# Fused attention and two expert stages: second products at four places of a unit, copies out of PSUM first in a step, the queries' split two steps sooner

## The chip, the cores and the metric

One core of one Trainium2 chip runs the whole program. The metric is device microseconds of one execution. The kernel before took 1058.69 us, the median of 3 runs (1058.37 to 1059.4).

## The reference

Attention over 4 batches, 8 heads, 576 positions and a head size of 64, with a bias that a small two-layer network makes of the relative position; then a dense layer with a rational activation, and a routed layer of 8 experts with one expert per token. Everything is fp32. Only attention bears on the change:

```
scores = q @ k.T / sqrt(64) + bias        # 576 x 576 for each batch and head
attn   = exp(scores - rowmax) / rowsum
out    = attn @ v                         # 576 x 64
h = out @ w_in ; g = rational(h) ; x = g @ w_out          # later stages, not touched
out[token] = gate * relu(x @ w1[e]) @ w2[e]
```

## The kernel before, in words

Attention handles two heads of one batch at a time. Such a pair is called a unit: 16 units, numbered u. A unit has nine steps, numbered j = 0 to 8: eight tiles of 128 queries, taken alternately from the two heads (`ORD`), and a ninth that holds the 64 remaining queries of both heads. The loop at L524 runs over all steps, `g = 9 * u + j`, and each turn issues work for several tiles at once, so that a tile passes through the engines over some turns. The order is written out by hand: nothing reorders it. Each engine takes its own instructions in that order, and waits at the head of its queue until what the instruction needs is there. TensorE is PE in the profile, VectorE is DVE, ScalarE is ACT, GpSimd is POOL, and SyncE (SP) issues the loads and stores.

In a turn the code issues, from the top:

- loads by SP: q and k of unit u + 2 at steps 0 to 5 (`load_unit`, L527), v at step 1 (`load_v`);
- `recip` of tile g - 3: on DVE an add and a reciprocal (L363, L364), on POOL a spread to 64 columns (`rb`, L366);
- `expo` of tile g - 2 on ACT (L351);
- `pend`: what the turn before has left to be copied out of PSUM. That is `stack_evac` (L297), `rest_evac` (L420) and `av_evac` (L440);
- `trans_pe` of tile g - 4 on PE (L393: the weights `e`, transposed; L396 and L397: a remainder and the reciprocals) and its copy out of PSUM by ACT (`trans_evac`, L370);
- `scores` of tile g on PE (L330);
- `stack_pe` on PE (L289, L291, L293, L294): q and k of the next unit are transposed, in five pieces that `STACK` assigns to steps 0, 1, 2, 3 and 7; their copies follow in the next turn: piece 4 by DVE (L302, L303), POOL (L304) and ACT (L305), pieces 0 and 2 by ACT (L307), pieces 1 and 3 by DVE (L310, L311);
- the second products, attention times v (`av_pe`, L436), for the unit before. Five chunks c of keys, for two ranges of queries: n = 0 (256 columns, steps in `AV0`) and n = 1 (320 columns, steps in `AV1`). They take 64 columns of the array for each head, and every product is two passes. After the last chunk DVE scales the result out of PSUM (`av_evac`, L445);
- `rowmax` of tile g - 1 on DVE (L346), which also frees the PSUM tile of the scores;
- `split_q` for unit u + 2 on POOL (L263, L265, L268): q is cut into a high and a low part, in four instructions;
- one part of the conversion of weights for a later stage (`CONV`, `conv`): on DVE L61, L62, L67, L70, L76, on ACT L65, on POOL L78 and L80 after L76, on SP loads and stores.

PSUM has two tiles of each kind. The transposes of `trans_pe` and `stack_pe` share the kind "tr": a unit asks for 14 of them in turn, so each needs the copy of the one before the last. In the order of a unit: T5 (the transposes of tile 5, issued in step 0), S4 (piece 4), T6, S0, T7, S1, T8, S2, T0, T1, T2, T3, S3, T4. T7 so needs T6's copy, and T5 needs S3's. Scores have the kind "sc" (a tile's scores need the `rowmax` of the tile two before), and the second products, the remainders and the reciprocals the kind "av".

Of the kernel before, what the change touches and what calls it, by code (L numbers as in the profile page):

```python
# [88 lines left out]
def attention(ctx, tc, k, ins):  # L89
# [121 lines left out]
    def load_bias(p, j):  # L211
        bt = ap.tile([P, S], F32, name="bias_s", bufs=11)
        t = ORD[j]
        for hd in (t // 4,) if t < 8 else range(2):

            n, lanes = (P, bt) if t < 8 else (S - 4 * P, bt[64 * hd:64 * hd + 64])
            r = t % 4 * P if t < 8 else 4 * P
            d = bias_d[r // P][0:n, 2 * p + hd, S - r:2 * S - r]
            for lo, hi, to in ((512, S, 0), (0, 512, 64)) if 4 <= t < 8 else ((0, S, 0),):
                nc.sync.dma_start(lanes[:, to:to + hi - lo], bass.AP(d.tensor, d.offset + lo, [[2 * H * S - 1, n], [1, hi - lo]]))  # L220
        bias_s[p, t] = bt

    def load(dst, src, hd, rem, near):

        if rem:
            nc.sync.dma_start(dst[64 * hd:64 * hd + 64, 8], src[512:576])
        else:
            load_chunks(dst[:, 4 * hd:4 * hd + 4], src[0:512], near)
# [8 lines left out]
    def load_unit(u, i):  # L237
        p, b = divmod(u, B)
        if i == 0:
            r = units[u] = K()  # L240
            r.u, r.p, r.b = u, p, b
            r.qn = xq.tile([P, 9, D], F32, name="qn")
            r.kn = xq.tile([P, 9, 2, D], F32, name="kn")
        r = units[u]
        hd, i = divmod(i, 3)
        dst, src = ((r.qn, ins["q"]), (r.kn[:, :, 0], ins["k"]), (r.kn[:, :, 1], ins["k"]))[i]
        for rem in range(2):
            load(dst, src[b, 2 * p + hd], hd, rem, i == 0)

    def load_v(u):  # L250
        r = units[u]
        r.vn = ap.tile([P, 8, D], F32, name="vn")
        for hd in range(2):
            h = 2 * r.p + hd
            load_chunks(r.vn[:, 4 * hd:4 * hd + 4], ins["v"][r.b, h, 0:512], True)
            nc.sync.dma_start(vrem[u % 2][64 * hd:64 * hd + 64, hd], ins["v"][r.b, h, 512:576])
# [92 lines left out]
    def expo(g):  # L349
        e, st = tiles[g][0:2]  # L350
        nc.scalar.activation(e, e, AF.Exp, bias=st[:, 0:1], scale=-1.0, accum_out=st[:, 1:2])  # L351
        if g % 9 == 8:
            both = tiles[g][3]
            nc.gpsimd.tensor_scalar(both[:, S:S + 64], e[:, 512:576], 1.0, 1.0, ALU.mult, ALU.mult)
# [3 lines left out]
    def recip(g):  # L358

        n = 1 if g % 9 == 8 else 2  # L360
        if g % 9 % 2 or n == 1:
            st = tiles[g][4]
            nc.vector.tensor_scalar(st[:, 2, 0:n], st[:, 1, 0:n], 1e-9, None, ALU.add)  # L363
            nc.vector.reciprocal(st[:, 3, 0:n], st[:, 2, 0:n])  # L364
            rb = recips[g] = ap.tile([P, 2, D], F32, name="rb")
            nc.gpsimd.tensor_scalar(rb, st[:, 3, 0:n].unsqueeze(2).to_broadcast([P, 2, D]), 1.0, 1.0, ALU.mult, ALU.mult)  # L366
# [8 lines left out]
    def trans_pe(g):  # L375
        u, j = divmod(g, 9)
        t = ORD[j]
        r = units[u]
        both = tiles[g][3]
        if j == 0:  # L380
            r.aT = [None, None]
            r.aR = [None, None]
            r.rem = [None, None]
        if j in (0, 4):
            w = Q1 if j == 0 else S - Q1
            n = j // 4
            r.aT[n] = ap.tile([P, 2, 4, w], F32, name=f"aT{n}", bufs=1)
            r.aR[n] = ap.tile([P, 2, w], F32, name=f"aR{n}", bufs=1)
            r.rem[n] = pst.tile([P, 512], F32, name="av")
        ps = r.tps = pst.tile([P, 512], F32, name="tr")  # L390
        for c in range(4):
            e0 = c // 2 * 2 * P + (640 if 4 <= t < 8 else 0)
            nc.tensor.transpose(ps[:, c * P:(c + 1) * P], both[:, e0 + c % 2:e0 + 2 * P:2], k.idf)  # L393
        if j % 2:
            n, q0 = t % 4 // 2, t % 2 * P
            nc.tensor.transpose(r.rem[n][:, Q1 + q0:Q1 + q0 + P], both[:, 512:640], k.idf)  # L396
            nc.tensor.transpose(r.rem[n][:, q0:q0 + P], recips.pop(g).rearrange("p a n -> p (a n)"), k.idf)  # L397
# [16 lines left out]
    def rest_pe(g):  # L414
        both = tiles.pop(g)[3]
        av0, rb = units[g // 9].av0, recips.pop(g)
        nc.tensor.transpose(av0[:, 384:512], both[:, 512:640], k.idf)
        nc.tensor.transpose(av0[:, 256:384], rb.rearrange("p a n -> p (a n)"), k.idf)
# [49 lines left out]
    def first_split(r, p):  # L468
        nc.gpsimd.tensor_scalar(r.xh[p], r.x[p], 1.0, 1.0, ALU.mult, ALU.mult)
        nc.vector.tensor_tensor(r.xl[p], r.x[p], r.xh[p].bitcast(F32), ALU.subtract)  # L470
# [45 lines left out]
    CONV = {0: [(6, -1), (8, -1), (1, 0), (2, 0)], 1: [(3, 0), (7, -1), (0, 1)], 2: [(4, 0)], 3: [(5, 0)], 4: [(6, 0)],  # L516
            5: [(1, 1), (8, 0)], 6: [(7, 0), (3, 1), (2, 1), (0, 2)], 7: [(4, 1)], 8: [(5, 1)]}
    STACK = {0: 4, 1: 0, 2: 1, 3: 2, 7: 3}
    SPLIT = {6: (0,), 7: (1,), 8: (2, 3)}
    AV0 = {0: (0, 1), 1: (2,), 2: (3, 4)}  # L520
    AV1 = {4: (0, 1), 6: (2,), 7: (3,), 8: (4,)}
    pend = []
    setup = routing_setup(tc, k, ins)
    for g in range(NG + 6):  # L524
        u, j = divmod(g, 9)
        if u + 2 < NU and j < 6:
            load_unit(u + 2, j)  # L527
        if 2 <= u < NU and j == 1:
            load_v(u)

        if u + 2 < NU and u % B == 2 and j in (3, 7):
            load_bias(u // B + 1, j // 4)
        w, i = divmod(g - 2, 9)
        if g > 2 and w % B == B - 1 and w + 1 < NU and i >= 2:
            load_bias(w // B + 1, i)
        if g == 3:
            load_bias(0, 8)
        if 12 <= g < 21 or g in (28, 30, 32, 34, 36):
            next(setup)
        if g in later:  # L540
            later[g]()
        if 0 <= g - 3 < NG:
            recip(g - 3)
        if 0 <= g - 2 < NG:
            expo(g - 2)
        for f in pend:
            f()
        pend = []
        if 0 <= g - LAG < NG:
            trans_pe(g - LAG)  # L550
            trans_evac(g - LAG)
        if g < NG:
            scores(g)
        if g - LAG >= 0 and (g - LAG) % 9 == 8 and g - LAG < NG:
            rest_pe(g - LAG)
            pend.append(lambda g=g: rest_evac(g - LAG))
        if u + 1 < NU and j in STACK:
            i = STACK[j]
            ps = stack_pe(u + 1, i)
            pend.append(lambda u=u, i=i, ps=ps: stack_evac(u + 1, i, ps))  # L560
        if 0 <= u - 1 < NU - 1 and j in AV1:
            for c in AV1[j]:
                av_pe(u - 1, 1, c)
            if j == 8:
                pend.append(lambda u=u: av_evac(u - 1, 1))
        if 0 <= g - 1 < NG:
            rowmax(g - 1)
        if u + 2 < NU and j in SPLIT:
            for i in SPLIT[j]:
                split_q(u + 2, i)  # L570
        v = u - 1
        if 0 <= v < NU and j in AV0:
            for c in AV0[j]:
                av_pe(v, 0, c)
            if j == 2:
                pend.append(lambda v=v: av_evac(v, 0))
        for part, d in CONV[j]:
            if 0 <= 2 * u + d < 32:
                conv(2 * u + d, part)
        if g == NG - 6:  # L580
            x0 = first_x()
        if NG - 4 <= g < NG:
            first_split(x0, g - (NG - 4))
        if NG <= g < NG + 3:
            first_mm(x0, g - NG)

        n = g - NG
        if n == 2:
            g_of_h = Rational(nc, k)
            for c in range(2):  # L590
                k.st[c].q = g_of_h.open(1, lambda name: ap.tile([P, S], F32, name="bias_s", bufs=11)[:, 0:k.NB].unsqueeze(1))
            q0, q1 = k.st[0].q, k.st[1].q
            g_of_h.first(q0, 0, k.st[0].h)
            g_of_h.den(q0)
            g_of_h.poly(q0, 0, k.st[0].h)
        if n == 3:
            g_of_h.inv(q0)
            g_of_h.first(q1, 0, k.st[1].h)
            g_of_h.den(q1)
            g_of_h.quot(q0)  # L600
        if n == 4:
            for c in range(5):
                av_pe(NU - 1, 1, c)
            av_evac(NU - 1, 1)
            g_of_h.high(q0, x0.g[0].unsqueeze(1))
            g_of_h.inv(q1)
            g_of_h.poly(q1, 0, k.st[1].h)
            g_of_h.low(q0, x0.g[1].unsqueeze(1))
            g_of_h.quot(q1)
            g_of_h.high(q1, x0.g[2].unsqueeze(1))  # L610
            g_of_h.low(q1, x0.g[3].unsqueeze(1))
# [964 lines left out]
```

## Time and profile before

| | |
|---|---|
| median of 3 runs | 1058.69 us |
| profiled execution, its own time | 1060.23 us |
| its span (first to last instruction) | 1058.5 us |
| busy: PE, PEld, DVE, ACT, POOL | 96%, 84%, 71%, 62%, 26% |
| units of attention | about 64 us to 380 us of the span |

Busy PE is not PE at its peak: its matmuls are pipelined and their ends are modelled. The weight loads (PEld) show better when PE was held: each matmul has one ahead of it. A "<-" names what ended the idle time ahead of an instruction; "issue" means nothing that the profile shows. In a timeline a row is the start, the duration and the instruction, with the number of equal ones that are drawn together; the starts of two rows that follow each other closely are the better measure of what an instruction costs its engine, since the durations overlap by up to 0.1 us.

### The profile page before, as it was taken

The page shows a single profiled execution, that of the slowest core. Times are in us where ns is not written, and L with a number is a line of the kernel's source. Part 1 is how long each engine was busy: PE and PEld are TensorE (multiplying, and loading weights), DVE is VectorE, ACT ScalarE, POOL GpSimd, SP SyncE. Part 2 cuts the span into 40 slices and gives each one's busy share as a digit, 9 for nine tenths or more (in the row PEclk, how much of TensorE's full clock was granted, in tenths as well). Part 3 has the DMA queues.
Part 4 walks back from the last instruction along what each step waited for, and adds up shares of the span by engine and source line. Part 5 has one row for each costly group of instructions (what it writes and reads, how often), then busy time and mean ns, then how long its engine had stood idle before and what let it go on. Part 6 is the DMA issues. An engine that isn't in the chain of part 4 may idle for free. (4 is left out here: it accounts for less than half of the span.)

```text
span 1058.5 us, 19117 instructions
## 1 busy us (share of the span) xinstructions
PE 1016.0 (96%) x6804; PEld 886.1 (84%) x6804; DVE 754.0 (71%) x1548; ACT 651.7 (62%) x1283; POOL 276.0 (26%) x445
## 2 busy tenths in 40 slices
PE   6989999999999999999999999999997999999995
PEld 4667777777777779999999999999997889999982
DVE  7988898888888858888888888888886522111210
ACT  6878788887888857676676767766764422222221
POOL 3434343344343210202103012021051443112200
PEclk9999999999999999999999999999998999999998
DMA  6886885774663318005103112042150366311100
GB/s 174 298 264 163 234 251 169 220 218 127 183 193 101 122 47 324 30 1 22 39 1 31 31 19 43 1 23 67 62 100 1 30 167 232 113 42 40 51 31 18
DMA packets 122072, 113.34 MB, mean 107 GB/s; under 512 B 65055, under 2 KB 94495, under 8 KB 121952
## 3 DMA queue, kind: packets, MB, share of 16 engines
q1 hardware_dynamic: 117828, 101.53, 35.8%
q0 software_dynamic: 3728, 10.25, 3.1%
q8 instruction: 61, 1.00, 0.4%
q14 instruction: 59, 0.48, 0.2%
q10 hardware_dynamic: 396, 0.08, 0.0%
HBM read 78.09 MB, written 33.79 MB: 106 GB/s over the span
## 5 line engine op out<-in xcount | busy, mean ns | idle before, releaser
L759 PE MATMUL sc<-gh,w_b 128*128 128x384 f32 x752 | 208.7, 338 | 1.2 <-ACT x L766 1.2
L759 PEld LDWEIGHTS sc<-gh,w_b 128*128 128x128 f32 x752 | 138.6, 189 | 1.8 <-ACT x L766 1.8
L759 PE MATMUL sc<-gl,w_b 128*128 128x384 f32 x376 | 127.1, 338 | 0.0
L393 PEld LDWEIGHTS tr<-idf,e 128*128 128x128 f32 x576 | 81.0, 207 | 49.1 <-issue 24.9
L351 ACT ACTIVATE e<-e,st 128x576 f32<-128x576 f32 x144 | 112.2, 779 | 14.1 <-DVE st L346 12.1
L370 ACT COPY aT<-tr 128x512 f32<-128x512 f32 x144 | 84.4, 586 | 44.5 <-PE tr L393 42.7
L346 DVE CUSTOM_DVE_ANT_0 e<-sc,bias_s 128x576 f32<-128x576 f32 x144 | 107.6, 748 | 5.4 <-PE sc L330 3.8
L1096 DVE SCALAR_TENSOR_TENSOR hl<-tr,hh 128x256 fp32r<-128x256 f32 x56 | 23.8, 425 | 121.5 <-ACT hh L1095 121.5
L671 PE MATMUL tr<-kn,w_a 128*128 128x384 f32 x372 | 107.0, 342 | 0.1
L393 PE MATMUL tr<-idf,e 128*128 128x128 f32 x576 | 105.1, 305 | 1.7 <-DVE kk L311 0.9
L330 PE MATMUL sc<-kk,qS 128*128 128x288 f32 x512 | 99.0, 315 | 0.4 <-DVE st L346 0.4
L660 ACT CAST gh<-t 128x768 fp32r<-128x768 f32 x47 | 39.2, 835 | 92.7 <-DVE t L656 92.7
L436 PE MATMUL av<-aT,vn 128*64 128x320 f32 (+1 forms) x512 | 82.8, 424 | 0.0
L1086 PE MATMUL tr<-kn,w_a 128*128 128x256 f32 x448 | 81.5, 280 | 0.8 <-DVE hl L1096 0.5
L330 PEld LDWEIGHTS sc<-kk,qS 128*128 128x128 f32 x512 | 72.9, 191 | 1.7 <-PE tr L289 0.5
L759 PEld LDWEIGHTS sc<-gl,w_b 128*128 128x128 f32 x376 | 71.1, 189 | 0.0
L1086 PEld LDWEIGHTS tr<-kn,w_a 128*128 128x128 f32 x448 | 69.7, 188 | 1.7 <-ACT w_b L1131 0.7
L1107 PE MATMUL sc<-w_a,hh 128*128 128x512 f32 x224 | 70.9, 393 | 0.0
L671 PEld LDWEIGHTS tr<-kn,w_a 128*128 128x128 f32 x372 | 68.0, 188 | 2.6 <-issue 2.3
L867 POOL DMA_INDIRECT tab<-ids,si x18 | 23.0, 1275 | 180.0 <-DVE cum L863 165.6
L366 POOL TENSOR_SCALAR rb<-st 128x128 f32<-128x128 f32 x80 | 23.9, 299 | 171.4 <-DVE st L364 155.9
L649 ACT ACTIVATE r<-q,one 128x768 f32<-128x768 f32 x47 | 44.1, 939 | 33.8 <-DVE q L645 33.8
(306 smaller groups left out, 2534.1 us busy)
## 6 DMA issues: line engine op xcount, KB each, us to landing
bias_d<-bo SPq DMA_DIRECT2D x36, 295.5 KB, 4.2
kn<-in_k_dram SPq DMA_DIRECT2D x64, 128.0 KB, 3.6
cst<-in_moe_w_out_dram SPq DMA_DIRECT2D x16, 512.0 KB, 3.9
wo_d<-cvw SPq DMA_DIRECT2D x16, 512.0 KB, 2.9
cst<-in_moe_w_in_dram SPq DMA_DIRECT2D x16, 512.0 KB, 4.8
w_b<-wo_d SPq DMA_DIRECT2D x16, 512.0 KB, 8.0
w_b<-in_moe_w_dram SPq DMA_DIRECT2D x16, 512.0 KB, 8.3
x_d<-xr SPq DMA_DIRECT2D x18, 256.5 KB, 11.7
```

The source lines that it names most:

```text
L330: nc.tensor.matmul(ps[:, hf, 0:HF], st, mv[:, hf * HF:(hf + 1) * HF], start=n == 0, stop=n == last)
L346: nc.vector.tensor_tensor_reduce(out=ev, in0=ps[:, :, 0:HF], in1=bv, scale=-1.0, scalar=3.0e38, op0=ALU.add, op1=ALU.min, accum_out=st[:, ...
L351: nc.scalar.activation(e, e, AF.Exp, bias=st[:, 0:1], scale=-1.0, accum_out=st[:, 1:2])
L370: nc.scalar.copy(dst, src)
L393: nc.tensor.transpose(ps[:, c * P:(c + 1) * P], both[:, e0 + c % 2:e0 + 2 * P:2], k.idf)
L436: nc.tensor.matmul(r.av[64 * hd:64 * hd + 64, 0:w], st, mv, start=c == 0, stop=c == 4)
L649: nc.scalar.activation(q.r, q.q, AF.Ln, bias=self.one[:, 0:1], scale=1.0)
L660: self.nc.scalar.copy(gh, q.t)
L671: nc.tensor.matmul(h[:, 0:k.NB], k.wi[f][:, wv, dc * P:(dc + 1) * P], xv[dc], start=n == 0, stop=n == 11)
L759: nc.tensor.matmul(r.acc[dc][:, 0:NB], wo[f][:, wv, ws], gv, start=f == 0 and n == 0, stop=f == NF - 1 and n == 2)
L1086: nc.tensor.matmul(ps[:, 0:n], w[:, wv, cs], xv[dc // 2][:, dc % 2], start=j == 0, stop=j == 11)
L1107: nc.tensor.matmul(r.acc[a], r.h[f][hv][:, cs], wa[8 + f][:, wv], start=f == 0 and n == 0, stop=f == 7 and n == 2)
```

## The change

Four tables and one order change. The second products of a unit are issued at four steps in place of seven: chunk 2 of range 0 goes from step 1 to step 0, and chunks 3 and 4 of range 1 go from steps 7 and 8 to step 6; the scaling of range 1 and the store that follows it come two turns sooner. The queries' split is issued at steps 4, 5, 6 and 7 in place of 6, 7 and 8, and for that the loads of both heads' q come at steps 0 and 1. The copies that the turn before has left (`pend`) stand ahead of `recip` and `expo`.

```
-    SPLIT = {6: (0,), 7: (1,), 8: (2, 3)}
-    AV0 = {0: (0, 1), 1: (2,), 2: (3, 4)}
-    AV1 = {4: (0, 1), 6: (2,), 7: (3,), 8: (4,)}
+    SPLIT = {4: (0,), 5: (1,), 6: (2,), 7: (3,)}
+    LOAD = (0, 3, 1, 2, 4, 5)
+    AV0 = {0: (0, 1, 2), 2: (3, 4)}
+    AV1 = {4: (0, 1), 6: (2, 3, 4)}
...
-            load_unit(u + 2, j)
+            load_unit(u + 2, LOAD[j])
...
             later[g]()
+
+        for f in pend:
+            f()
+        pend = []
         if 0 <= g - 3 < NG:
             recip(g - 3)
         if 0 <= g - 2 < NG:
             expo(g - 2)
-        for f in pend:
-            f()
-        pend = []
...
-            if j == 8:
+            if j == 6:
                 pend.append(lambda u=u: av_evac(u - 1, 1))
```

## Rows read from the trace of the kernel before

**Rows 1.** Windows: stretch, its length, each engine's busy us, PEclk, DMA share, GB/s.
```profile
200.00:300.00 100.00, 99.69 (x731) 76.02 (x729) 85.86 (x234) 80.52 (x182) 40.43 (x76) 1.00 0.65 184
```

**Rows 2.** Timeline of PEld, one unit: start, us, instruction, idle before and releaser.
```profile
301.16 0.56 PEld L393 LDWEIGHTS tr<-idf,e 128*128 128x128 f32 x4 [0.38 <-issue]
...
303.25 0.55 PEld L393 LDWEIGHTS tr<-idf,e 128*128 128x128 f32 x4 [0.39 <-issue]
...
308.17 0.58 PEld L330 LDWEIGHTS sc<-kk,qS 128*128 128x128 f32 x4
...
310.15 0.56 PEld L393 LDWEIGHTS tr<-idf,e 128*128 128x128 f32 x4 [0.49 <-ACT qS L307]
...
310.84 0.56 PEld L330 LDWEIGHTS sc<-kk,qS 128*128 128x128 f32 x4
311.35 0.57 PEld L393 LDWEIGHTS tr<-idf,e 128*128 128x128 f32 x4
311.83 0.58 PEld L330 LDWEIGHTS sc<-kk,qS 128*128 128x128 f32 x4
...
313.26 0.56 PEld L393 LDWEIGHTS tr<-idf,e 128*128 128x128 f32 x4 [0.49 <-ACT aT L370]
...
314.46 0.49 PEld L291 LDWEIGHTS tr<-idf,kn 128*128 128x128 f32 x4
...
318.94 0.56 PEld L330 LDWEIGHTS sc<-kk,qS 128*128 128x128 f32 x4
...
320.84 0.56 PEld L393 LDWEIGHTS tr<-idf,e 128*128 128x128 f32 x4 [0.39 <-issue]
```

**Rows 3.** Timeline of DVE in the same unit.
```profile
312.36 0.69 DVE L67 SCALAR_TENSOR_TENSOR cvt<-cst,cvt 128x512 uint32<-128x512 uint32 x1
...
315.23 0.69 DVE L310 CAST kk<-tr 128x512 fp32r<-128x512 f32 x1 [0.62 <-PE tr L291]
...
318.38 0.49 DVE L445 TENSOR_TENSOR xs<-av,aR 128x320 f32<-128x320 f32 x1 [0.73 <-PE av L436]
...
319.46 0.42 DVE L61 TENSOR_SCALAR cvt<-cst 128x512 uint32<-128x512 uint32 x1
319.92 0.69 DVE L62 SCALAR_TENSOR_TENSOR cvt<-cst,cvt 128x512 uint32<-128x512 uint32 x1
```

**Rows 4.** Timeline of DVE from step 8 of unit 0 to step 1 of unit 1.
```profile
77.76 0.67 DVE L310 CAST kk<-tr 128x512 fp32r<-128x512 f32 x1
...
79.07 0.75 DVE L346 CUSTOM_DVE_ANT_0 e<-sc,bias_s 128x576 f32<-128x576 f32 x1
...
80.79 0.48 DVE L61 TENSOR_SCALAR cvt<-cst 128x512 uint32<-128x512 uint32 x1
81.30 1.11 DVE L62 SCALAR_TENSOR_TENSOR cvt<-cst,cvt 128x512 uint32<-128x512 uint32 x1
82.33 0.15 DVE L363 TENSOR_SCALAR st<-st 128x2 f32<-128x2 f32 x1
...
82.91 0.29 DVE L303 TENSOR_TENSOR kk<-tr,kk 128x128 fp32r<-128x128 f32 x1
```

**Rows 5.** Timeline of POOL in that stretch.
```profile
80.25 0.74 POOL L78 TENSOR_TENSOR cvw<-cvt,cvw 128x256 fp32r<-128x256 f32 x1 [0.42 <-DVE cvw L76]
80.94 0.92 POOL L80 TENSOR_TENSOR cvw<-cvt,cvw 128x256 fp32r<-128x256 f32 x1
```

**Rows 6.** Timeline of ACT in that stretch.
```profile
81.69 0.78 ACT L351 ACTIVATE e<-e,st 128x576 f32<-128x576 f32 x1
...
83.29 0.27 ACT L305 CAST qrem<-tr 128x128 fp32r<-128x128 f32 x1 [0.74 <-DVE kk L303]
83.45 0.59 ACT L370 COPY aT<-tr 128x512 f32<-128x512 f32 x1
```

**Rows 7.** Timeline of PEld in that stretch: piece 0 behind L305.
```profile
83.61 0.40 PEld L289 LDWEIGHTS tr<-idr,qs 128*128 128x128 f32 x4 [0.19 <-ACT qrem L305]
```

**Rows 8.** Source line L305, all 16 units: what ended ACT's idle time before it (us, times).
```profile
  DVE kk L303: 10.0, 16
```

## The prediction

> **What bounds the kernel now.** I read the page first (the table above): PE is busy 96% of the span, and the change touches only attention, so next the windows. In a window of mid-attention [rows 1] PE shows 99.69 of 100 us, but its weight loads only 76.02, DVE 85.86 and ACT 80.52; the granted clock is 1.00. PE's figure hides gaps, so I went to the timeline of the weight loads over one unit [rows 2]. The unit starts with T6's loads at 301.16 and comes round at 320.84: 19.68 us. The idle times in it are only those beside second products, 0.38 or 0.49 ahead of the next transposes, always the same size, whatever the profile names as releaser ("issue", an ACT copy). So these are no waits for another engine: PE runs through its queue at its own pace, and PE bounds the unit. DVE is the next busiest, and waits for PE at two kinds of places [rows 3]: L310 for the transposes of k (0.62), L445 for the second products (0.73). Last I looked at who stands close behind PE: ACT's L305 waits for DVE's L303 in all 16 units [rows 8], and PE's piece S0 waits for L305 in the first of them, starting 0.05 after its end (83.56 to 83.61) [rows 6, 7].
>
> **Part 1, fewer places.** From scores to the next transposes PE takes 0.51 us with no second products between (310.84 to 311.35), 1.43 with one chunk (311.83 to 313.26), 1.98 with two (308.17 to 310.15) [rows 2]. A chunk so costs 0.55 and a place 0.92 - 0.55 = 0.37 beside it. Three places go, and I take the same 0.37 for the one with 256 columns: 1.11 us less in a unit of PE, 18.57, if nothing else holds it. The chunks themselves stay and move: 0.55 each from steps 7 and 8 to step 6, about 0.43 (0.55 x 256 / 320, an estimate) from step 1 to step 0. Their inputs are ready by then, since the last copies into aT and aR come in step 4 at the latest.
>
> What moves with them: L445 now stands at the head of DVE's step 7 and waits for three chunks. T3 would come at 313.26 + 2 x 0.55 = 314.36 on the clock of rows 2, while L67 of step 6 is done at 313.05 [rows 3], so DVE stands idle some 1.3 us. Behind L445 queue the `rowmax` of tile 6 (L346), L70 and L310. Nobody needs these sooner than L310 needs S3: S3 is 1.20 behind T3 [rows 2], L310 0.77 behind S3's start (314.46 to 315.23) [rows 2, 3], together 1.97; the three in front take 0.49 + 0.75 + 0.69 = 1.93 [rows 3, 4] (L70 taken like L67). So this wait costs nothing, but it leaves nothing over. The stores of the result are issued earlier on SP, with no reader inside attention.
>
> **Part 2, what PE runs into.** Steps 7, 8 and 1 lose their second products on PE, and DVE's work there stays. I follow it from S3 (step 7) to the next thing that PE needs from it.
>
> S3's start to L310: 0.77. L310 to the end of L303: in the first unit DVE runs through just this list without a wait (L310, L311, `rowmax` 7, L76, `rowmax` 8, L61, L62, one add and reciprocal, L302, L303), from 77.76 to 82.91 + 0.29 = 83.20: 5.44 us [rows 4]. The new order puts one `recip` in (behind L311) and one out (behind L303), equal ones, so 5.44 stays. L305 starts 0.09 later, the next ACT instruction 0.16 after it [rows 6]. In the new order that one is the exponential of tile 8, 0.78, and only then comes the copy of T6, 0.59 [rows 6]. PE follows 0.05 behind a copy [rows 7]. Sum 0.09 + 0.16 + 0.78 + 0.59 + 0.05 = 1.67. T7 needs T6's copy, as the tr tiles go in turn. From T7 to the next S3 PE's queue takes 314.46 - 303.25 = 11.21 [rows 2], and with two chunks more 12.31. The circle S3, DVE, ACT, T7, S3 is 0.77 + 5.44 + 1.67 + 12.31 = 20.19 us. That is more than PE's 18.57 and 0.51 more than the 19.68 of before.
>
> The same stretch holds PE once more, inside the circle: scores of step 0 need `rowmax` 7, which ends 0.77 + 1.31 (77.76 to 79.07) + 0.3 (add and reciprocal; 82.33 to 82.91, less L302) + 0.75 = 3.13 after S3's start [rows 2 to 4], 3.18 with the 0.05; PE would be there after 318.94 - 314.46 = 4.48 less two places of 0.92, 2.64. This 0.54 adds nothing, since T6 still ends before ACT gets to its copy.
>
> **Part 3, copies first.** Of the 1.67 above, the exponential's 0.78 is new: before, it stood ahead of L305 and filled ACT's wait for L303. On DVE, L302 gains the time of a `recip`, 0.3. In steps 2 and 4 ACT's copies (L307, `rest_evac`) come sooner by one exponential, which nothing waits for now (no PE idle time beyond the fixed ones [rows 2]). Net, 0.5 worse, in the circle.
>
> **Part 4, split and loads.** POOL is busy 40.43 of 100 us [rows 1]. Four instructions move two steps ahead; the transposes that read them come in the next unit. They now stand ahead of L78 and L80 in steps 4 and 5, so L61 and L67 of steps 5 and 6 may find POOL at work; up to some 0.4 each (below), hidden in the 1.3 us at L445. SP issues as many loads as before in other order; q is there three steps ahead of the split, and k of the first head comes a step or two later for use in the next unit. I take 0; without that cover it would be up to 0.8 a unit.
>
> **The term I had to choose.** L61 and L62 in step 0 took 1.62 us in the first unit (80.79 to 82.41) [rows 4], 1.15 in a later one (319.46 to 320.61) [rows 3]. In the first unit L78 and L80 were running beside them, L80 itself 0.92 in place of 0.74 [rows 5]; in the later one L445's wait had let POOL finish. L78 starts behind L76, and in the new order L76, `rowmax` 8 and L61 stand back to back as in the first unit, so I take 1.62. The ends are 1.15 (circle 19.72) and L61 waiting for both POOL instructions: L61 starts 0.54 after L78, the two last 0.69 + 0.74, and L61 ends 0.28 behind (81.27 against 80.99), so 1.89 with L62 (circle 20.46).
>
> The Trainium skill ("SBUF — State Buffer", section "Who interferes with whom") says that VectorE and GpSimd share a pair of SBUF ports as an exclusive lock for a whole instruction, and counts VectorE instructions with two SBUF inputs in. The trace agrees: L62 took 1.11 beside L80 and 0.69 alone. By that rule the circle is 20.19 or 20.46, without it 19.72.
>
> **Sum.** The trace is of an execution of 1060.23 us (span 1058.5), 1.5 above the median; attention's units in it are regular, so the difference is put on the median. Fourteen passages between units 1 and 15 at +0.51: +7.1. The first passage already has the crowded pattern: 0. The last unit has no S3, and keeps the three places' gain: -1.1. Together +6.0: 1064.7 (1066.2 on the profiled execution's own scale).
>
> **Rivals.**
> - *T7 is not held, PE stays the bound (faster).* It decides at one place: whether T6's copy is done when PE has finished S0. For: ACT has 20% idle time [rows 1]. Against: the wait of L305 for L303 in every unit [rows 8], with the exponential behind it. If only the scores' wait of 0.54 stays, the unit is 18.57 + 0.54 = 19.11 and 15 units give 8.6: 1050.1; if nothing stays, 15 x 1.11 = 16.7: 1042. The Trainium skill ("TensorEngine Tiling (Array Packing)", "Key Properties") says that changing the tiling mode drains TensorE. By it each place removed pays whatever the neighbours do, which is the 1042; the fixed 0.37 a place agrees.
> - *POOL is out of the way in step 0 (no change).* Circle 19.72: 14 x 0.04 - 1.1 = -0.5, 1058.2. For: 1.15 is the row of most later units' shape. Against: it came with DVE's wait at L445, which moves to step 7.
> - *POOL goes first with both (slower still).* Circle 20.46: 14 x 0.78 - 1.1 = +9.8, 1068.5.
>
> **Chances.** Forecast 0.54, POOL first 0.12, POOL away 0.17, T7 not held 0.17. Changes under 0.2% (2.1 us) can't be told from none here. Slower 0.65, the first two; same 0.17; faster 0.18. The range reaches from below the case without POOL to above the heavy one and leaves out the faster rival: 1056 to 1070; the likeliest case alone has 1062 to 1068.
>
> **What would show it.** Right: T7's loads (L393 in step 2) with 0.4 to 1 us of idle time and an ACT copy as releaser; scores of step 0 behind L346; L62 of step 0 near 1.1; L445 in step 7 with more than 1 us of wait; a unit near 20.2. Wrong: no idle time ahead of T7 and a unit near 18.6 to 19.1 (parts 2 and 3 fall), or L62 of 0.69 in step 0 with a unit near 19.7 (only the chosen term falls).

## The result, and the profile after

The changed kernel took 1066.05 us (median of 4 runs, 1065.95 to 1067.82) against 1058.53 for the kernel before in the same runs: ratio 1.0069, 95% interval 1.0053 to 1.0084. It is slower by 7.5 us; the forecast was 1064.7. The profiled execution took 1065.97 us, 5.7 above the one of before.

PE is still busy nearly all the time by the page, and spends less on second products, but the window of mid-attention now shows it held: PE 95.47 of 100 us where [rows 1] have 99.69, and DVE 91.11 where they have 85.86.

```profile
200.00:300.00 100.00, 95.47 (x714) 75.24 (x712) 91.11 (x229) 78.29 (x180) 44.17 (x75) 1.00 0.64 181
```

The timeline of the weight loads (start, duration, instruction, idle time before it and releaser), from step 7 of one unit to T7 of the next and on to the next S3, answers to [rows 2]:

```profile
301.39 0.49 PEld L291 LDWEIGHTS tr<-idf,kn 128*128 128x128 f32 x4
...
303.36 0.58 PEld L393 LDWEIGHTS tr<-idf,e 128*128 128x128 f32 x4
303.85 0.15 PEld L396 LDWEIGHTS av<-idf,e 128*128 128x128 f32 x1
304.36 0.14 PEld L397 LDWEIGHTS av<-idf,rb 128*128 128x128 f32 x1 [0.36 <-POOL rb L366]
304.56 0.56 PEld L330 LDWEIGHTS sc<-kk,qS 128*128 128x128 f32 x4
...
306.90 0.56 PEld L393 LDWEIGHTS tr<-idf,e 128*128 128x128 f32 x4 [0.38 <-ACT cvq L65]
...
308.07 0.40 PEld L289 LDWEIGHTS tr<-idr,qs 128*128 128x128 f32 x4
309.31 0.56 PEld L393 LDWEIGHTS tr<-idf,e 128*128 128x128 f32 x4 [0.84 <-ACT aT L370]
...
321.61 0.49 PEld L291 LDWEIGHTS tr<-idf,kn 128*128 128x128 f32 x4
```

T7 (309.31) sat idle 0.84 us behind ACT's copy. In step 0, T5's last part (L397, 304.36) waited 0.36 behind POOL's spread reciprocals. From S3 to S3 it is 321.61 - 301.39 = 20.22 here; the median over units 10 to 14 is in the table of the next section.

The other side of the circle, DVE, then ACT, then POOL in the same stretch; these answer to [rows 4], [rows 6] and [rows 5].

```profile
302.16 0.69 DVE L310 CAST kk<-tr 128x512 fp32r<-128x512 f32 x1
...
303.49 0.16 DVE L363 TENSOR_SCALAR st<-st 128x2 f32<-128x2 f32 x1
...
303.76 0.74 DVE L346 CUSTOM_DVE_ANT_0 e<-sc,bias_s 128x576 f32<-128x576 f32 x1
...
304.43 0.42 DVE L76 CAST w_a<-cvt 128x512 fp32r<-128x512 f32 x1
...
305.44 0.55 DVE L61 TENSOR_SCALAR cvt<-cst 128x512 uint32<-128x512 uint32 x1
306.02 1.12 DVE L62 SCALAR_TENSOR_TENSOR cvt<-cst,cvt 128x512 uint32<-128x512 uint32 x1
...
307.37 0.29 DVE L303 TENSOR_TENSOR kk<-tr,kk 128x128 fp32r<-128x128 f32 x1
```
```profile
307.75 0.27 ACT L305 CAST qrem<-tr 128x128 fp32r<-128x128 f32 x1 [1.28 <-DVE st L363]
307.92 0.78 ACT L351 ACTIVATE e<-e,st 128x576 f32<-128x576 f32 x1
...
308.69 0.57 ACT L370 COPY aT<-tr 128x512 f32<-128x512 f32 x1
```
```profile
304.01 0.30 POOL L366 TENSOR_SCALAR rb<-st 128x128 f32<-128x128 f32 x1 [3.58 <-DVE st L364]
304.93 0.74 POOL L78 TENSOR_TENSOR w_a<-cvt,w_a 128x256 fp32r<-128x256 f32 x1 [0.62 <-DVE w_a L76]
305.63 0.96 POOL L80 TENSOR_TENSOR w_a<-cvt,w_a 128x256 fp32r<-128x256 f32 x1
```

S3 to L310 0.77, L310 to the end of L303 (307.66) 5.50, L305 0.09 later, then 0.17, 0.77, 0.57 and 0.05 to T7: 1.65 for the five. T7 to S3 321.61 - 309.31 = 12.30. The forecast's four terms were 0.77, 5.44, 1.67 and 12.31. The profile names L363 as L305's releaser, where [rows 8] name L303; L305 still starts 0.09 behind L303's end, so I read the same wait, with L363 merely running beside it by then. The scores of step 0 (304.56) start 0.06 behind the end of `rowmax` 7 (L346, 303.76 + 0.74).

### The profile page after: what moved, and what is told of

Same layout as the page of the kernel before. It is cut to its first block, busy times and chain, and to the rows that moved or that the text cites. A ratio compares the mean times of both kernels' runs of the same rounds, so it can differ in the third digit from the quotient of the medians.

```text
span 1064.2 us, 19112 instructions
## 1 busy us (share of the span) xinstructions
PE 1009.7 (95%) x6804; PEld 890.3 (84%) x6804; DVE 775.8 (73%) x1548; ACT 648.2 (61%) x1283; POOL 289.5 (27%) x445
## 5 line engine op out<-in xcount | busy, mean ns | idle before, releaser
L393 PEld LDWEIGHTS tr<-idf,e 128*128 128x128 f32 x576 | 81.2, 206 | 39.3 <-ACT aT L370 19.0
L393 PE MATMUL tr<-idf,e 128*128 128x128 f32 x576 | 101.3, 299 | 10.7 <-ACT aT L370 9.9
L346 DVE CUSTOM_DVE_ANT_0 e<-sc,bias_s 128x576 f32<-128x576 f32 x144 | 107.1, 745 | 2.3 <-PE sc L330 1.4
L370 ACT COPY aT<-tr 128x512 f32<-128x512 f32 x144 | 83.7, 581 | 31.8 <-PE tr L393 30.3
L436 PE MATMUL av<-aT,vn 128*64 128x320 f32 (+1 forms) x512 | 76.0, 418 | 0.0
L656 DVE SCALAR_TENSOR_TENSOR t<-t,coef,r 128x768 f32<-128x768 f32 x47 | 47.6, 1014 | 24.2 <-ACT r L652 24.2
```

Of the source, the lines that this page charges most:

```text
L346: nc.vector.tensor_tensor_reduce(out=ev, in0=ps[:, :, 0:HF], in1=bv, scale=-1.0, scalar=3.0e38, op0=ALU.add, op1=ALU.min, accum_out=st[:, ...
L370: nc.scalar.copy(dst, src)
L436: nc.tensor.matmul(r.av[64 * hd:64 * hd + 64, 0:w], st, mv, start=c == 0, stop=c == 4)
L656: nc.vector.scalar_tensor_tensor(q.t, q.t, co[:, 0:1], q.r, ALU.add, ALU.mult)
```

## The experiments

Units 10 to 14 are regular in all runs, so one table shows where PE's time went: from the first load of a step's transposes (L393) to the first of the next, median over these units, in us. The last column is the whole unit, and depends by a few hundredths on the step from which it is counted. Units 2 and 3 are longer in all runs and unit 8 in several (20.45, 20.46 and 20.38 in the kernel before, by the `rowmax` of tile 0), so a run's time does not move by 15 times the change of its unit. The row of the kernel before is PE undisturbed. Steps 2, 4 and 5, and with the new places 6, 7 and 8, agree within 0.04 in all runs but the last, so only steps 0, 1 and 3 tell something. Undisturbed, the four places would have about 2.61 + 0.43 = 3.04 in step 0 (run 10, where nothing waits there, has 3.05) and 1.43 in step 1 (as in runs 3, 9 and 10), so 18.7 in all.

```
                                   step 0  1     2     3     4     5     6     7     8     unit
before                             2.61  2.09  2.87  1.59  2.44  1.20  1.91  2.55  2.43  19.68
changed                            3.55  2.37  2.88  1.59  2.44  1.20  2.98  1.66  1.51  20.17
1 changed, order of before         3.40  1.88  2.91  1.59  2.44  1.20  2.98  1.66  1.51  19.58
2 before, copies first             2.61  2.54  2.87  1.59  2.44  1.20  1.91  2.55  2.43  20.14
3 changed, L61 and L62 in step 1   3.55  1.43  2.88  1.77  2.43  1.21  2.98  1.66  1.51  19.41
4 changed, split of before         4.35  2.58  2.88  1.59  2.44  1.20  2.98  1.66  1.51  21.19
5 changed, L78 and L80 in step 1   3.55  1.86  2.88  1.59  2.44  1.20  2.98  1.66  1.51  19.67
6 changed, one exponential moved   3.55  1.62  2.87  1.60  2.44  1.21  2.98  1.66  1.51  19.43
7 before, copies and split moved   2.61  2.09  2.87  1.59  2.44  1.20  1.91  2.55  2.43  19.68
8 before, four places only         3.37  1.88  2.91  1.59  2.44  1.20  2.98  1.66  1.51  19.54
9 as 1, with L61 and L62 moved     3.40  1.43  2.88  1.76  2.43  1.20  2.98  1.66  1.51  19.27
10 as 9, with S3 in step 5         3.05  1.43  2.88  1.59  2.44  1.66  2.97  1.21  1.53  18.76
```

Theory: the circle of the prediction sets the unit. Rival 1: what costs is L445's wait at the head of DVE's step 7. Rival 2: what costs is the earlier split's work on POOL. The runs are told in the order of the argument. Runs 1 to 4, 5 to 7 with 9, and 8 with 10 were compared with the kernel before on the same chip each, with medians of 1060.07, 1060.47 and 1060.43 for it.

**Run 6: one exponential.**
```
+        if j == 1 and 0 <= g - 2 < NG:
+            expo(g - 2)
         for f in pend:
...
-        if 0 <= g - 2 < NG:
+        if j != 1 and 0 <= g - 2 < NG:
             expo(g - 2)
```


> The changed kernel with one instruction moved: in step 1 alone the exponential stands ahead of the copies, as before. Theory: T6's copy comes 0.78 sooner, step 1 of PE falls from 2.37 to about 1.6, the unit from 20.17 to 19.4; about 11 us less than the changed kernel. Rival 1 and Rival 2 (L445's wait, POOL's split): no change, 20.17.

Measured 1059.43 us, ratio to the kernel before 0.9989 (0.9973 to 1.0005). The unit is 19.43, step 1 is 1.62, 0.19 above undisturbed, and the profile lists no idle time ahead of T7's loads (301.62) any more:

```profile
300.01 0.56 PEld L393 LDWEIGHTS tr<-idf,e 128*128 128x128 f32 x4 [0.39 <-ACT cvq L65]
...
301.13 0.40 PEld L289 LDWEIGHTS tr<-idr,qs 128*128 128x128 f32 x4
301.62 0.56 PEld L393 LDWEIGHTS tr<-idf,e 128*128 128x128 f32 x4
```

One instruction's place on an engine that is idle a fifth of the time is worth 0.74 us a unit. The time is about 8.5 us below the changed kernel's by the two ratios, where 11 was expected: units 2 and 3 gain less (20.95 to 20.61 and 21.32 to 21.18), and unit 8 is longer (20.23 to 20.65). Rivals 1 and 2, which had no change here, fall as the cause of this part.

**Run 5: the collision with POOL, in half of the units.**
```
+            late = part in (6, 8) and d == -1 and j == (0 if u > 8 else 1)
-            if 0 <= 2 * u + d < 32:
+            if 0 <= 2 * u + d < 32 and not late:
```
with parts 6 and 8 listed in both steps of `CONV`.

> The changed kernel, but from unit 9 on L78 and L80 of step 0 are issued in step 1, behind the exponential's copy; units 1 to 8 are as changed. Theory: the collision is a term of the circle, so L62 of step 0 falls from 1.11 to 0.69 and the later units from 20.17 to about 19.7, while the earlier ones stay at 20.17; 7 units at 0.47 make about 3 us. Rival 1 (L445's wait) and the rival that PE is held by the spread reciprocals alone (L397 behind rb): all units 20.17.

Measured 1062.89 us, ratio 1.0030 (1.0016 to 1.0044). By the `rowmax` of tile 0, the starts of units 5 to 8 lie 20.18 to 20.21 apart, those of units 8 to 14 19.66 to 19.74. L62 of DVE in step 0 of unit 7 in this run, then of unit 12:

```profile
204.48 1.11 DVE L62 SCALAR_TENSOR_TENSOR cvt<-cst,cvt 128x512 uint32<-128x512 uint32 x1
...
303.83 0.69 DVE L62 SCALAR_TENSOR_TENSOR cvt<-cst,cvt 128x512 uint32<-128x512 uint32 x1
```

The 0.47 that the prediction chose for the collision is measured as 20.18 - 19.67 = 0.51, within one execution. Rival 1, and the rival that L397's wait alone holds PE, had all units alike, and fall for this part.

**Run 3: L61 and L62 out of the circle.**
```
-    CONV = {0: [(6, -1), (8, -1), (1, 0), (2, 0)], 1: [(3, 0), ...
+    CONV = {0: [(6, -1), (8, -1), (2, 0)], 1: [(1, 0), (3, 0), ...
```


> The changed kernel with L61 and L62 of step 0 issued in step 1, ahead of L67. Theory: 1.65 us leave the circle (20.18 to 18.5), so that PE with the scores' wait of 0.54 sets the unit: 19.1, some 15 us less, 1050 to 1052, faster than the kernel before. Rival 1 (L445's wait): DVE has the same work and the same wait, 1066. Rival 2 (POOL): only the 0.47 of the collision with L80 goes, 1059 to 1060.

Measured 1058.31 us, ratio 0.9988 (0.9977 to 0.9999), unit 19.41. Step 1 falls to 1.43, undisturbed, as the theory has it. The size was missed by 0.3 a unit, and with it the time (1050 to 1052 expected): PE's own pace is 18.7 and not 18.57, and step 3 takes 1.77 for 1.59. There S2's loads (287.43) start 0.05 behind the end of ACT's copy of T8 (L370, 286.79 + 0.59), for which they wait here and in run 9; in all other runs they start before it ends. Why they wait for it in these two is not shown. Step 0 stays at 3.55, as expected. The time alone does not tell the theory from rival 2 (1059 to 1060), step 1 does: it falls by 0.94, and the collision is worth 0.51 (run 5).

**Run 1: the order of before.** In the changed kernel, `pend` stands behind `recip` and `expo` again.

> The changed kernel with the copies put back behind recip and expo; the four places and the earlier split stay. Theory (the circle S3, DVE, L305, exponential, copy of T6, T7): the exponential leaves the circle, 20.18 - 0.78 = 19.40 us a unit, T7 still held but by about 0.1 to 0.3; 14 units give 11 us: about 1055. Rival 1 (L445 at the head of step 7 is what costs, since DVE idles there): the wait stays, so 1066. Rival 2 (POOL's split beside L61, L62, L67 and ahead of the spread reciprocals is what costs): it stays too, 1066.

Measured 1059.96 us, ratio 0.9996 (0.9981 to 1.0010), unit 19.58 against 19.40 expected, and the time 5 us above the forecast of about 1055. L397 no longer waits and T7 hardly, but S0 is held 0.4 by L305, and the scores of step 0 0.3 by `rowmax` 7. What the forecast of this run left out is that a `recip` now stands ahead of L310, which starts 0.90 after S3 (297.36 to 298.26) in place of 0.77. The order's 0.59 a unit goes; the rivals' terms, left in, don't bring it back.

**Run 2: the order alone.** This is the kernel before with `pend` ahead of `recip` and `expo`.

> The kernel before with only the copies put ahead of recip and expo. Theory: the order costs only where the circle binds. Here step 1 still has its second products, T6's copy would end at 321.12 + 1.62 = 322.74 on the clock of rows 2 and T7 needs it at 322.93, so it is just covered: 1058 to 1059, a unit of 19.68. Rival (the order costs by itself, 0.5 a unit): 1066.

Measured 1067.38 us, ratio 1.0078 (1.0059 to 1.0096), unit 20.14. Here my theory was wrong and its rival right in the number. DVE, then POOL, from step 8 on:

```profile
301.31 0.16 DVE L363 TENSOR_SCALAR st<-st 128x2 f32<-128x2 f32 x1
...
302.25 0.99 DVE L76 CAST w_a<-cvt 128x512 fp32r<-128x512 f32 x1
...
304.85 1.10 DVE L62 SCALAR_TENSOR_TENSOR cvt<-cst,cvt 128x512 uint32<-128x512 uint32 x1
```
```profile
301.82 0.30 POOL L366 TENSOR_SCALAR rb<-st 128x128 f32<-128x128 f32 x1 [3.49 <-DVE st L364]
302.09 1.75 POOL L268 TENSOR_TENSOR qs<-qt,qs 128x320 fp32r<-128x320 f32 x2
303.80 0.73 POOL L78 TENSOR_TENSOR w_a<-cvt,w_a 128x256 fp32r<-128x256 f32 x1
304.50 0.91 POOL L80 TENSOR_TENSOR w_a<-cvt,w_a 128x256 fp32r<-128x256 f32 x1
```

`recip` (L363) has slipped behind L311, so POOL's spread (L366) is later, and the two subtractions of the split behind it in POOL's queue come up beside L76, which takes 0.99 for 0.42, and push L78 and L80 beside L61 and L62. I had followed the moved copies on ACT and DVE, and not the `recip` that they displace through POOL.

**Run 7: copies first with the earlier split, places of before.** This tells apart the exponential in any place from the collision.

> The kernel before with the copies first and the earlier split and loads, its seven places kept. The order alone gave 20.14 a unit, with POOL's subtractions of the split (L268) running beside L76 and pushing L80 beside L62 in step 8 and 0. Theory after that run: it is this collision that makes the order dear where PE has its old places, and the earlier split removes it: 19.68 to 19.75, as the kernel before. Rival (the exponential ahead of T6's copy costs in any case): 20.1.

Measured 1060.86 us, ratio 1.0011 (1.0000 to 1.0021), unit 19.68, the steps of the kernel before to the hundredth. So the order costs nothing while PE's step 1 keeps its second products and POOL is out of the way (L76 takes 0.42 and L62 0.69 here, at 298.06 and 300.48); in run 2 it was the collision. The rival of both runs falls. The loads moved together with the split, here and in run 4, and no run has one without the other; what stands beside L76 in the traces is the split's L268.

**Run 4: the split at its old steps.** `SPLIT` and the loads of before in the changed kernel.

> The changed kernel with the split and the loads at the steps of before; places and order as changed. Theory: the split's earlier steps cost nothing; back in step 8 its two subtractions come up beside L76 and push L78 and L80 further beside L61 and L62, so the circle gets 0 to 0.7 longer: 1066 to 1075. Rival 2 (the earlier split costs): faster, 1058 to 1062. Rival 1 (L445's wait): 1066 in either case.

Measured 1082.29 us, ratio 1.0207 (1.0190 to 1.0224), unit 21.19. The direction is as expected, the size above the range: beside POOL both L76 (0.99) and L61 (0.96) take longer, for 0.42 and 0.55 in the changed kernel, and L62 as long as there (1.10). From L310 to the end of L303 it is 6.48 (293.00 to 299.48) for 5.50, which is 0.98 of the 1.02 by which the unit is longer.

```profile
295.27 0.99 DVE L76 CAST w_a<-cvt 128x512 fp32r<-128x512 f32 x1
...
296.86 0.96 DVE L61 TENSOR_SCALAR cvt<-cst 128x512 uint32<-128x512 uint32 x1
297.85 1.10 DVE L62 SCALAR_TENSOR_TENSOR cvt<-cst,cvt 128x512 uint32<-128x512 uint32 x1
```

Step 0's 4.35 shows a second wait that the late split brings: the transposition of the remaining queries (L294) waits for the split itself.

```profile
296.90 0.14 PEld L294 LDWEIGHTS tr<-idr,qs 128*128 128x128 f32 x1 [0.85 <-POOL qs L268]
```

T7 waits 0.84 for ACT's copy all the same (301.13), so this wait lies inside the circle, like that of the scores, and adds nothing to it. The earlier split, rival 2's culprit, is worth 1.0 us a unit in this order (21.19 to 20.17).

**Run 8: the four places alone.** `AV0`, `AV1` and the step of `av_evac` of the change in the kernel before.

> The kernel before with only the four places (order, split and loads as before). Theory: the circle without the exponential in it, as with the old order and the earlier split (19.58), but POOL's subtractions of the split come beside L76 in step 8 again: 19.6 to 20.1 a unit, so between the kernel before and 5 us slower; the 1.02 that PE saves does not come out. Rival (the places alone bring PE's saving, and order or split took it away): 18.7 a unit, 14 us faster.

Measured 1056.79 us, ratio 0.9971 (0.9959 to 0.9983), unit 19.54. The places alone are faster than the kernel before, by 0.14 of the 1.0 that PE saves (19.68 to 18.7). The unit is just below the range expected (19.6 to 20.1). Against my expectation the split's subtractions don't meet L76 here: with `recip` ahead of L310 they are nearly through when it starts, and it takes its 0.42. S0 (0.34 behind L305) and the scores of step 0 (0.28 behind `rowmax` 7) take the rest.

```profile
296.93 0.56 PEld L330 LDWEIGHTS sc<-kk,qS 128*128 128x128 f32 x4 [0.28 <-DVE st L346]
...
300.66 0.39 PEld L289 LDWEIGHTS tr<-idr,qs 128*128 128x128 f32 x4 [0.34 <-ACT qrem L305]
```

**Run 9: what the others point to.** The order of before and run 3's move, with four places and the earlier split.

> Four places and the earlier split, the order of before, and L61 and L62 of step 0 in step 1. Theory: nothing holds T7 and S0 any more; what stays is the scores of step 0 behind rowmax 7 (0.3 to 0.5): 19.0 to 19.2 a unit against 19.68 before, 6 to 10 us below the kernel before. Rival (DVE as a whole is the bound now, which the places' gain can't pass): 19.4 or more, no more than 4 below.

Measured 1056.27 us, ratio 0.9958 (0.9941 to 0.9975), unit 19.27. T7 and S0 run free; 0.36 in step 0 (the scores behind `rowmax` 7) and 0.17 in step 3 stay, where S2 waits for ACT's copy of T8, as in run 3. The expectation was missed: the unit is above 19.0 to 19.2, and the time 4.2 us below the kernel before in place of 6 to 10. So this run alone does not rule out its rival, DVE as a whole.

**Run 10: S3 out of step 8's way.** In addition
```
-    STACK = {0: 4, 1: 0, 2: 1, 3: 2, 7: 3}
+    STACK = {0: 4, 1: 0, 2: 1, 3: 2, 5: 3}
```


> Four places, earlier split, order of before, L61 and L62 in step 1, and in addition piece 3 of the transposes (S3) issued in step 5 in place of 7, so that L310 and L311 leave DVE's step 8. Theory: the last hold, the scores of step 0 behind rowmax 7, goes: 18.7 to 18.9 a unit, 10 to 14 us below the kernel before. Rival (DVE as a whole is by then the bound): 19.2 or more, no better than the run without this move (19.27).

Measured 1051.43 us (1048.80 to 1052.31), ratio 0.9911 (0.9892 to 0.9930), unit 18.76: faster than both kernels, and in units 10 to 14 within 0.1 of PE's own pace. The scores of step 0 follow the transposes without idle time, though DVE is busy 91.77 of 100 us in this run:

```profile
200.00:300.00 100.00, 98.65 (x756) 79.42 (x755) 91.77 (x243) 82.68 (x189) 46.51 (x80) 1.00 0.69 194
```
```profile
295.63 0.14 PEld L397 LDWEIGHTS av<-idf,rb 128*128 128x128 f32 x1
295.74 0.56 PEld L330 LDWEIGHTS sc<-kk,qS 128*128 128x128 f32 x4
```

So DVE's total was not the limit in run 9; where in the unit its work stands was. The time is 9.0 us below the kernel before, short of the 10 to 14 expected, because units 2, 3, 4 and 8 still take 20.3 to 20.8. In units 4 and 8 DVE waits for the conversion's transfers, in unit 4 L76 for 2.20 (152.00) and in unit 8 L61:

```profile
232.51 0.43 DVE L61 TENSOR_SCALAR cvt<-cst 128x512 uint32<-128x512 uint32 x1 [3.23 <-DMA cst<-in_moe_w_in_dram]
```

In the kernel before L61 waits there too, 1.95, and starts at 232.48: this load comes no sooner when the units ahead of it get shorter.

## Why the prediction held, point by point

- *PE bounds the unit before, and a place costs 0.37 beside its chunks.* Held: the undisturbed steps give 18.7 where the prediction had 18.57. The place with 256 columns was priced like the others: step 1 loses 2.09 - 1.43 = 0.66, of which 0.43 is the chunk, so 0.23 and not 0.37.
- *The circle is 20.19.* Held in the sum and in each of its four terms (first section), and its parts one by one: the exponential 0.74 (run 6), the collision 0.51 (run 5), L61 and L62 together (run 3 frees T7). The Trainium skill's exclusive lock ("SBUF — State Buffer", "Who interferes with whom") stands with run 5: the same instruction 1.11 beside L80 and 0.69 without it.
- *The scores of step 0 come 3.18 after S3, behind `rowmax` 7.* The time held: 304.56 - 301.39 = 3.17. The place was not the whole of it: L397 in front of them waits for POOL's spread reciprocals, because `recip` went behind L311. I had not followed this one from DVE through POOL to PE. `rowmax` 7 ends later than the spread (304.50 against 304.31), so it cost nothing here; in run 2 the same omission made my expectation wrong by 0.46 a unit.
- *DVE idles 1.3 us at L445.* It does where the split keeps its old steps (1.40 in run 8, at 292.84). In the changed kernel it is 0.48 (300.33 in this trace) or 0.49 a unit later, so the sign that asked for more than 1 us of wait did not come:

```profile
316.42 1.03 DVE L62 SCALAR_TENSOR_TENSOR cvt<-cst,cvt 128x512 uint32<-128x512 uint32 x1
317.38 0.70 DVE L363 TENSOR_SCALAR st<-st 128x2 f32<-128x2 f32 x1
...
318.91 1.14 DVE L67 SCALAR_TENSOR_TENSOR cvt<-cst,cvt 128x512 uint32<-128x512 uint32 x1
320.55 0.49 DVE L445 TENSOR_TENSOR xs<-av,aR 128x320 f32<-128x320 f32 x1 [0.49 <-PE av L436]
```
  The earlier split in steps 5 and 6, and L80 that it pushes back, cost L62 0.34, L363 0.54 and L67 0.45, where the prediction had up to 0.8 in all. The idle time covered these 1.3 us with 0.5 to spare, so part 4's zero held.
- *Copies first is net 0.5 worse.* Held for the changed places: 20.17 against 19.58 without it (run 1). The same change of order costs 0.46 at the old places with the late split (run 2), 0.00 with the earlier one (run 7), and 1.65 at the changed places with the late split (19.54 to 21.19, runs 8 and 4), so it has no price of its own.
- *The sum.* The profiled executions differ by 5.7, the sum said 6.0. That it came so close is in part luck, since two misses cancel. By the `rowmax` of tile 0, the start of unit 0 to that of unit 15 is 7.7 longer (7.1 expected: the first unit was 0.46 longer, not equal), and what follows gives 2.0 back, not 1.1. Of these 2.0, 1.0 falls within unit 15 (15.98 to 14.97 up to its last `rowmax`), where the forecast had 1.1. The other 1.0 falls behind attention, where the stretch after the last `rowmax` takes 682.3 in the kernel before and 681.3 in the changed one; the work there is the same in all runs, and takes 680.1 to 684.7 in the others, so this part can't be told from the spread. The medians differ by 7.5; the kernel before's profiled execution was 1.5 above the median that the prediction started from, the changed kernel's at its median.
- *The chances.* The two slower cases add up to 0.66, not 0.65; nothing hangs on it.

## What to carry to other kernels

When an engine that bounds a loop gives up time in some steps, walk from there through the other queues until the next thing that it needs, and add up that circle: here 20.19 us against 18.57 of PE's own work told the result before it was run. A change of order has no price by itself; it costs where it puts an instruction into that circle, and it moves what stands behind it on the other queues too (the `recip` here, through GpSimd). After that, take work out of the circle rather than out of the engine: the four places alone gave 0.3% (run 8), and with L61, L62 and S3 with its two copies moved out of the circle's stretch 0.9% (run 10, which has the earlier split too).

## What the runs showed of the hardware that was not expected

An add on 128x2 elements (L363) took 0.70 us beside POOL's L80, 0.16 alone: even a DVE instruction of this size can lose 0.54, more than three times its own length. It works both ways: L80 took 1.17 there and 0.74 alone, and L354, a POOL copy of 64 columns, 0.44 beside L67 for 0.24 alone. Reductions out of PSUM (L346, 0.75) and copies out of PSUM (L310, L311, 0.69) kept their time beside POOL in all runs (0.73 to 0.76 and 0.67 to 0.69).
